# Norms on GpSimd, key blocks in four column tiles, loads by use and chunks of five in a fused attention and Mish kernel

## The chip, the cores and the metric

The kernel runs on 1 core of one Trainium2 chip. The metric is the device time in microseconds of one execution; the time before is the median of three runs, 1579.51 us (1578.79 to 1581.96). The engines are called PE (TensorE), DVE (VectorE), ACT (ScalarE), POOL (GpSimd) and SP (SyncE, which here issues the DMAs). PEld is PE's loading of weights.

## The reference

Everything is FP32. S = 2048 rows of D = 512, 32 query heads of 16 that share one key and one value head, and a hidden layer of F = 1792.

```python
xn = layernorm(x)                                   # no gain, no bias
q  = (xn @ wq) as 32 heads of 16;  k = xn @ wk;  v = xn @ wv
p  = softmax(q @ k.T / 4)                           # over all 2048 keys
s  = concat_heads(p @ v) @ wo
h  = xn @ w1 + b1
g  = silu((h * tanh(softplus(h))) @ w2)             # Mish between two products
out = x + s * g
```

## The kernel before

**Precision.** Most operands are kept as a high and a low FP32R part (`hi_pool` or an ACT copy makes the high part, `sub` the low one), and a product of two such operands is three PE products (`TERMS`). The key and value projection is done in plain FP32 with `wkf`, a weight tile in which the key's 16 columns are repeated six times, columns 48 to 63 are zero, and the value's 16 stand last; the trace shows each FP32 product as two records.

**Work units.** Rows are handled in four chunks of 512 (c = 0 to 3), and heads in sets of four. `NU = 32` pairs of chunk and head set, each with 16 key tiles, make `NS = 512` steps s. In a step, `e_one` makes four score products (`e`) that ACT turns into exponentials (`pt`), `m_one` makes some four products (`m`) whose maxima DVE takes for a later set (`mb`), and `pv` adds the `pt` of two steps before to the output, as four column tiles of 32.

**Groups.** Between these, PE works through *groups* of products that share one PSUM bank (`xps`): a query block (12 products, `q_group`), a block of the first factor (12, `m1_group`), a third of a second-factor product (15, 15 and 12, `m2_groups`), an output block (12, `wo_groups`). `queue` holds them in order, `qqueue` the query groups with the steps from which they may begin; `begin` takes the first that is ready, and goes past a waiting output group to the next first-factor group. `waves` puts one chunk of a group into two steps: the upper halves of its products (64 rows of the contraction) in one, the lower halves in the other, each beside `e` and `m` products that use the other half of PE's rows. `chunk_size` cuts a group into equal chunks of at most `XMAX = 8`, so 12 are 6 + 6 and 15 are 8 + 7; either way a group takes four steps. `m_sides` decides how many `m` stand on which side. After the maxima are all taken, 20 steps (`LEAD`) before the end, the last steps run in pairs with two groups at a time.

**Weights.** `items` has a list for each tag: `wq` (query), `ws` (first factor), `wb` and `wx` (second factor and output). `load` issues the next load of a tag when its place in the ring is free and one of two raw buffers is; `pump` calls it for every tag in the order of the dictionary (wq, ws, wb, wx), and the lead-in's planner does the same. `split` makes the two parts: in the lead-in with an ACT copy and a subtraction on POOL, later both on POOL. Split weights are kept in DRAM and come back ready in later chunks.

**The lead-in.** Before step 0 a planner writes the order of all engines by hand: tasks with an engine, a duration, what they depend on and a priority; at each turn the task that can start first is issued (`best`). `norm_a`, `norm_b` and `norm_c` turn a chunk's sums into `rstd` and `nbias` (DVE, ACT, DVE); DVE gathers the sums of chunks 0 to 2 (`stats`), ACT those of chunk 3 (`stats_a`). `x_scale` applies them, `x_transpose` turns the tiles on PE, `x_copy` brings them to `xf`. Then `k_proj` makes key block c with four accumulating products; `k_high` (ACT) and `k_low` (DVE) write the keys `ks`, `v_copy`, `v_transpose` and `v_out` the values. `m` products of a key block can begin when its `k_low` is done (`kready`); the order over query set and key block is in `MSEQ`. Where PE would wait more than 0.35 us, it does three products of a group ("X"; one group more may begin per 13 us after 18 us) or a warm-up product that nobody reads (`keep_warm`). The lead-in ends when 40 `m` products on each half are out and the row maxima of the first set have been moved (`c_rows`).

Of the kernel before, what the change touches and what calls it, by code (L numbers as in the profile page):

```python
# [14 lines left out]
F32 = mybir.dt.float32  # L15
# [65 lines left out]
class Item:  # L81
    def __init__(self, tag, key, src):
        self.tag, self.key, self.src = tag, key, src
        self.raw = self.tile = None
        self.step = None
        self.users = 0


class Group:
    def __init__(self, mms, post, items=(), after=(), pre=None, start=None, wo=None, alloc=None):  # L90
        self.mms, self.post, self.items, self.after, self.pre = mms, post, items, after, pre
        self.start, self.wo, self.alloc = start, wo, alloc
        self.done = None
        self.m1 = None
        self.dve = False
        self.per = None
        for i in items:
            i.users += 1
# [26 lines left out]
def block_kernel(ctx: ExitStack, tc: tile.TileContext, x, wq, wk, wv, wo, w1, b1, w2, out):  # L125
# [127 lines left out]
    def norm_a(z):  # L253
        if z.start >= A_LO:
            dve.tensor_scalar(ve[:, z], mvs[:, z, 1], 1.0 / D, EPS, op0=ALU.mult, op1=ALU.add)
        else:
            dve.tensor_scalar(ve[:, z], mvs[:, z, 1], EPS, None, op0=ALU.add)
# [5 lines left out]
    def norm_c(z):  # L263
        r, h = rstd[:, z], hv[:, z]
        stt(h, ve[:, z], -0.5, r, ALU.mult, ALU.mult)
        mul(dve, h, h, r)
        stt(r, h, 1.5, r, ALU.add, ALU.mult)
        if z.start >= A_LO:
            mul(dve, nbias[:, z], nbias[:, z], r)
        else:  # L270
            stt(nbias[:, z], mvs[:, z, 0], -1.0, r, ALU.mult, ALU.mult)
# [39 lines left out]

    kp_of = {}
    vp_of = {}

    def k_proj(c, dts):
# [15 lines left out]
    def v_copy(c):  # L331
        vt_of[c] = sb.tile([P, C], F32, tag=f"y{(2, 3, 1, 2)[c]}", name=f"vt{c}", bufs=1)[0:32]
        act.activation(vt_of[c], kp_of[c][96:128], AF.Copy)
# [9 lines left out]
    load_x(0)  # L343
    wkv = sb.tile([P, C], F32, tag="qf", name="wkv", bufs=1)
    wkv = wkv[:, 0:2 * NDT * DH].rearrange("p (a t n) -> p a t n", a=2, t=NDT)
    sp.dma_start(wkv[:, 0], wk.rearrange("(t p) n -> p t n", p=P))
    sp.dma_start(wkv[:, 1], wv.rearrange("(t p) n -> p t n", p=P))
    for j in range(8):
        if j != 3:
            pool.tensor_copy(wkf[:, :, DH * j:DH * (j + 1)], wkv[:, j // 7])  # L350

    timed = {}
# [103 lines left out]
    def load(tag):  # L456
# [14 lines left out]
        elif n - k < NRAW[tag] and raws[-RAWS] is not None and raws[-RAWS] <= step[0]:  # L471
# [8 lines left out]
            todo[tag][1] += 1  # L480

    def pump():
        for tag in items:
            while arrived(tag):
                split(tag)
            load(tag)

# [8 lines left out]
    def prepare():  # L496
        for n in range(min(2 if step[0] < NS - LEAD else 8, len(queue))):
            if queue[n].pre and queue[n].pre():
                queue[n].pre = None

    def begin():
        prepare()
# [10 lines left out]
        if g.start:  # L513
            g.start()
        if g.alloc:
            ps = g.alloc()
        else:
            ps = ps_x.tile([P, 512], F32, tag="x", name="xps")
# [114 lines left out]

    def chunk_size(n):
        return -(-n // -(-n // XMAX)) if n else 0

    def waves(h, em, new):
# [4 lines left out]
        if not cur["chunk"] and (not new or cur["g"] is None and not begin()):  # L642
            mms = []
        else:
            g = cur["g"]
            mms = cur["chunk"] or g.mms[cur["n"]:cur["n"] + chunk_size(len(g.mms) - cur["n"])]
        second = bool(cur["chunk"])
# [6 lines left out]
        xs = deque(mms)  # L654
        swap = k % 2 and not second
        relay = None
# [346 lines left out]
    for c in range(NC):  # L1003
        for k in range(3):
# [13 lines left out]
            queue.extend(g2)  # L1018
    queue.extend(wo_groups(NC - 1))

    pt_of = {}
# [50 lines left out]
    def m_sides(h, k, second):  # L1072

        tot = 4 + (0 if k % 2 == 0 else -1 if second else 1)
        tot = min(tot, 64 * NU - sum(m_next))
# [5 lines left out]
        if k == 6 and abs(off) > 1:  # L1081
            n -= 1 if off > 0 else -1
        n = max(min(n, hi), lo)
        return n, tot - n
# [217 lines left out]
    for c0, c1 in ((0, 1), (1, 2), (2, 3), (3, 4)):  # L1302
        z = slice(4 * c0, 4 * c1)
        na = task("DVE", 0.2, lambda z=z: norm_a(z), st[z], prio=c0 and 1)
        nb = task("ACT", 0.45, lambda z=z: norm_b(z), [na])
        nrm = task("DVE", 0.8, lambda z=z: norm_c(z), [nb], prio=2 * c0 and 1)
        for c in range(c0, c1):
# [39 lines left out]
            kus = 0.9  # L1347
            k0 = kp = task("PE", kus, lambda c=c: k_proj(c, (0,)), xs)
            for dt in range(1, 4):
                kp = task("PE", kus, lambda c=c, dt=dt: k_proj(c, (dt,)), [kp], lat=0.0)  # L1350
            kv_done = kp
# [37 lines left out]
    while True:  # L1389
# [24 lines left out]
        when(s)  # L1414
        for tag in items:
            load(tag)
# [31 lines left out]
        elif k == "J":  # L1448
# [5 lines left out]
            else:  # L1454
                gap[0] = 0
                if not plan["POOL"]:
                    act_jobs(1)
# [29 lines left out]
    for s in range(NS + 2000):  # L1487
        inm = s < NS - LEAD
        if inm or cur["chunk"]:
# [4 lines left out]
            def em(k, second):  # L1494
# [3 lines left out]
                r = [[], []]  # L1498
                for op in EM if k % 2 == 0 or second else EM[::-1]:
                    if op == "M" and y:  # L1500
# [67 lines left out]
```

## Time and profile before

| | before |
|---|---|
| median of 3 runs | 1579.51 us |
| the profiled execution's own time | 1578.89 us |
| its span | 1577.1 us |
| granted PE clock | 1.000 |
| PE, DVE, ACT, POOL busy | 99%, 85%, 83%, 40% of the span |
| the first set of `pv` products | at 87.01 us |

A busy row of the profile gives, for a group of instructions, the line, the engine, the operation, what is written from what, and the count; then the busy time in us and the mean duration in ns. A row of the timeline gives the start and the time that it spans in us, then the same; what ended the engine's idle time before it stands in square brackets. A stretch gives its length and then the busy time of each engine with its number of instructions.

### The profile page before, as it was taken

What the parts mean: (1) busy time and instruction counts of PE and PEld (TensorE: products, weight loads), DVE (VectorE), ACT (ScalarE), POOL (GpSimd) and SP (SyncE); (2) the same over time, 40 slices, a digit from 0 to 9 for tenths busy, and PEclk for the clock granted to TensorE, in tenths of its full rate; (3) what the DMA queues carried; (4) which work ended last, traced back from release to release, by engine and by line L of the source; (5) the groups of instructions that cost most, each with busy time, mean ns of one, the idle gap of its engine ahead of it and who ended that gap; (6) DMA issues with size and microseconds to landing.
All of it is one profiled execution on the core that took longest, in us unless ns stands there. A gap on an engine that the chain in (4) does not pass through costs nothing.

```text
span 1577.1 us, 31648 instructions
## 1 busy us (share of the span) xinstructions
PE 1565.6 (99%) x11717; PEld 842.5 (53%) x11717; DVE 1343.6 (85%) x2339; ACT 1306.6 (83%) x2515; POOL 627.5 (40%) x641
## 2 busy tenths in 40 slices
PE   9999999999999999999999999999999999999998
PEld 5455555555555555555555555555555555555554
DVE  8998888889989888888998988888889998888832
ACT  7588788798998778878989887887898878789886
POOL 3476266275474105503515320471251515126412
PEclk9999999999999999999999999999999999999999
DMA  6333231142321314122032232221332213032020
GB/s 195 94 118 112 65 99 44 55 125 85 121 93 48 102 33 149 45 69 81 26 99 66 60 97 68 84 60 26 116 98 85 74 40 110 19 111 58 15 81 28
DMA packets 74666, 124.31 MB, mean 79 GB/s; under 512 B 21520, under 2 KB 35344, under 8 KB 74512
## 3 DMA queue, kind: packets, MB, share of 16 engines
q1 hardware_dynamic: 74512, 122.29, 25.1%
q8 instruction: 93, 1.52, 0.4%
q14 instruction: 61, 0.50, 0.1%
HBM read 74.78 MB, written 26.21 MB: 64 GB/s over the span
## 4 chain that ended last, share of the span: by engine, by line
PE 96%; DVE 3%; ACT 1%; DMA 0%; issue 0%; SPq 0%; ACTq 0%; DVEq 0%
PE xps L118 44%; PE pv L1126 32%; PE e L1039 9%; PE m L1060 8%; DVE mb L1064 2%; PE kp L319 1%; PE xps L114 0%; PE late L118 0%; ACT pt L1041 0%; PE xp L287 0%; PE late L1039 0%; DMA xin<-in_dram 0%; PE wop L118 0%; PE late L114 0%; PE wop L114 0%
## 5 line engine op out<-in xcount | busy, mean ns | idle before, releaser
L1064 DVE TENSOR_REDUCE mb<-m 128x1 f32<-128x512 f32 x2048 | 1274.2, 683 | 172.2 <-PE m L1060 148.8
L1041 ACT ACTIVATE pt<-e 128x512 f32<-128x512 f32 x2018 | 1061.7, 602 | 221.1 <-PE e L1039 213.3
L1060 PE MATMUL m<-ks,qt 48*128 48x512 f32 (+1 forms) x2048 | 830.3, 420 | 1.3 <-DVE mb L1064 0.4
L1039 PE MATMUL e<-qt,ks 64*128 64x512 f32 x2018 | 740.4, 401 | 0.5 <-ACT pt L1041 0.3
L1126 PE MATMUL pv<-pt,vaug 128*32 128x512 f32 x4096 | 543.0, 604 | 0.0
L1060 PEld LDWEIGHTS m<-ks,qt 48*128 48x128 f32 (+1 forms) x2048 | 372.4, 185 | 59.5 <-DVE mb L1064 21.5
L1039 PEld LDWEIGHTS e<-qt,ks 64*128 64x128 f32 x2018 | 373.1, 186 | 17.1 <-ACT pt L1041 5.7
L118 PE MATMUL xps<-wbs,act 64*128 64x512 f32 x1248 | 338.1, 407 | 0.2
L118 PEld LDWEIGHTS xps<-wbs,act 64*128 64x128 f32 x1248 | 217.5, 185 | 173.9 <-ACT pt L1041 101.6
L118 PE MATMUL xps<-xt,ws 64*128 64x512 f32 x1104 | 306.1, 410 | 0.3 <-DVE y L851 0.2
L118 PEld LDWEIGHTS xps<-xt,ws 64*128 64x128 f32 x1104 | 190.2, 185 | 182.7 <-ACT pt L1041 116.5
L172 POOL TENSOR_SCALAR t<-t 128x512 f32<-128x512 f32 x56 | 34.5, 616 | 400.3 <-ACT t L784 400.1
L1126 PEld LDWEIGHTS pv<-pt,vaug 128*32 128x32 f32 x4096 | 81.8, 108 | 137.9 <-issue 129.6
L162 POOL TENSOR_TENSOR hb<-hb,t 128x512 f32<-128x512 f32 x56 | 72.2, 1289 | 69.2 <-ACT t L797 54.2
L118 PE MATMUL xps<-xt,wq 64*128 64x512 f32 x336 | 93.1, 410 | 0.0
L118 PEld LDWEIGHTS xps<-xt,wq 64*128 64x128 f32 x336 | 57.9, 185 | 55.4 <-ACT pt L1041 35.2
L118 PE MATMUL xps<-wbs,ot_all 64*128 64x512 f32 x288 | 79.5, 408 | 0.0
L118 PEld LDWEIGHTS xps<-wbs,ot_all 64*128 64x128 f32 x288 | 49.5, 184 | 46.7 <-ACT pt L1041 29.3
L162 POOL TENSOR_TENSOR hb<-hb,u 128x512 f32<-128x512 f32 x56 | 72.4, 1292 | 4.4
L162 POOL TENSOR_TENSOR u<-u,t 128x512 f32<-128x512 f32 x56 | 71.9, 1284 | 4.7
L162 POOL TENSOR_TENSOR act<-hb,act 128x512 fp32r<-128x512 f32 x55 | 70.9, 1290 | 4.6
L157 POOL TENSOR_SCALAR qh<-qf 128x512 fp32r<-128x512 f32 x15 | 9.3, 622 | 104.8 <-ACT qf L716 69.4
(146 smaller groups left out, 959.4 us busy)
## 6 DMA issues: line engine op xcount, KB each, us to landing
wbs<-w SPq DMA_DIRECT2D x36, 512.0 KB
ws<-w SPq DMA_DIRECT2D x35, 512.0 KB
qt<-qh SPq DMA_DIRECT2D x256, 32.0 KB
wq<-wq SPq DMA_DIRECT2D x14, 512.0 KB
w<-wbs SPq DMA_DIRECT2D x14, 512.0 KB
wbs<-wo SPq DMA_DIRECT2D x12, 512.0 KB
rawws<-in_dram SPq DMA_DIRECT2D x21, 256.0 KB
rawwb<-in_dram SPq DMA_DIRECT2D x20, 256.0 KB
```

The source lines that it names most:

```text
L118: i = self.pe.matmul(ps, self.lhs()[o], self.rhs()[o], start=(self.k == 0 and self.halves == 0), stop=(self.k == self.tot - 1 and self.hal ...
L157: pool.tensor_scalar(o, i, 1.0, 0.0, op0=ALU.mult, op1=ALU.add)
L162: eng.tensor_tensor(out=o, in0=a, in1=b, op=op)
L172: pool.tensor_scalar(o, o, lim, 0.0, op0=ALU.min, op1=ALU.max)
L319: pe.matmul(kp_of[c], wkf[:, dt], xf_of[c][dt // 2][:, dt % 2], start=(dt == 0), stop=(dt == 3))
L1039: pe.matmul(e, ks[o:o + 64, P * k:P * (k + 1)], q[o:o + 64, p], start=True, stop=True)
L1041: r = act.activation(pt, e, AF.Exp, scale=0.25)
L1060: pe.matmul(m, q[o, p, P * t:P * (t + 1)], ks[o, C * kb:C * (kb + 1)], start=True, stop=True)
L1064: r = dve.reduce_max(out=mb_of[v][:, kb, z:z + 1], in_=m, axis=AX.X)
L1126: pe.matmul(o[32 * j:32 * j + 32], vaug[:, k], pt, start=(k == 0), stop=(k == 15))
```

## The change

It has four parts.

1. **Norms.** For chunks 2 and 3 `norm_a` and `norm_c` are issued on POOL, as products of two tensors and scalar operations, and the planner has them as POOL tasks. Where the planner held timed work and jobs back while POOL had any task, it now does so while one is due.
2. **Key blocks 1 to 3.** `k_part` makes, for each half of 256 columns, four products at once, one for each quarter of the contraction, each into 32 rows of one bank (the last 32 columns of `wkf`: 16 of the key, 16 of the value). `k_stage` copies the bank to SBUF on ACT, and `k_sum` adds the four quarters and repeats the key with one product by a matrix of identity blocks, `ksum`. POOL makes this matrix from the identity with a memset and 28 small copies. Block 0 stays as it is.
3. **Loads by use.** Each item gets the number of the first group in the queue that uses it (`use`; query items 8n − 7), and `load` is called for the tags in the order of their next item's number.
4. **Fives.** When a group of 15 begins while the groups before the first output group of chunk 0 leave more than one step to spare (`spare_steps`), it is cut into three chunks of five. `m_sides` and the order in a step treat five as an even number: four `m`, two on each side.

```diff
+        self.use = 0
+        self.most = XMAX
     def norm_a(z):
-        if z.start >= A_LO:
+        if z.start >= 8:
+            charge(0.25)
+            pool.tensor_scalar(ve[:, z], mvs[:, z, 1], 1.0 / D if z.start >= A_LO else 1.0, EPS, op0=ALU.mult, op1=ALU.add)
+        elif z.start >= A_LO:
...
     def norm_c(z):
-        r, h = rstd[:, z], hv[:, z]
+        r, h, b = rstd[:, z], hv[:, z], nbias[:, z]
+        if z.start >= 8:
+            charge(1.1)
+            pool.tensor_tensor(out=h, in0=ve[:, z], in1=r, op=ALU.mult)
+            pool.tensor_tensor(out=h, in0=h, in1=r, op=ALU.mult)
+            pool.tensor_scalar(h, h, -0.5, 1.5, op0=ALU.mult, op1=ALU.add)
+            pool.tensor_tensor(out=r, in0=h, in1=r, op=ALU.mult)
+            if z.start < A_LO:
+                pool.tensor_scalar(b, mvs[:, z, 0], -1.0, 0.0, op0=ALU.mult, op1=ALU.add)
+            pool.tensor_tensor(out=b, in0=b, in1=r, op=ALU.mult)
+            return
...
+    def k_part(c):
+        kq = ps_v.tile([P, C], F32, tag="v", name=f"kq{c}")
+        for h in range(2):
+            z = slice(C // 2 * h, C // 2 * (h + 1))
+            for dt in range(NDT):
+                pe.matmul(kq[32 * dt:32 * dt + 32, z], wkf[:, dt, P - 32:P], xf_of[c][dt // 2][:, dt % 2, z], start=True, stop=True)
+        kq_of[c] = kq
+
+    def k_stage(c):
+        vt_of[c] = sb.tile([P, C], F32, tag=f"y{(2, 3, 1, 2)[c]}", name=f"vt{c}", bufs=1)
+        act.activation(vt_of[c], kq_of[c], AF.Copy)
+
+    def k_sum(c):
+        kp_of[c] = ps_v.tile([P, C], F32, tag="v", name=f"kp{c}")
+        pe.matmul(kp_of[c], ksum, vt_of[c], start=True, stop=True)
...
+    ksum = wkv[:, P:2 * P]
...
+    pool.memset(ksum, 0.0)
+    for dt in range(NDT):
+        for j in range(8):
+            if j != 3:
+                pool.tensor_copy(ksum[32 * dt:32 * dt + 32, DH * j:DH * (j + 1)], ident[32 * dt:32 * dt + 32, 32 * dt + DH * (j // 7):32 * dt + DH * (j // 7 + 1)])
...
+    def by_use():
+        return sorted(items, key=lambda g: items[g][todo[g][1]].use if todo[g][1] < len(items[g]) else 10 ** 6)
+
     def pump():
         for tag in items:
             while arrived(tag):
                 split(tag)
+        for tag in by_use():
             load(tag)
...
+    def spare_steps():
+
+        n = next((n for n, g in enumerate(queue) if g.wo is not None), None)
+        if n is None or queue[n].wo:
+            return 0
+        due = 16 * 8 * (queue[n].wo + 1) + 9
+        return due - step[0] - 13 - 4 * (1 + n + sum(32 * (16 - k) - LEAD - 20 < due for k in range(1, len(qqueue) + 1)))
...
+        if len(g.mms) == 15 and spare_steps() > 1:
+            g.most = 5
...
-    def chunk_size(n):
-        return -(-n // -(-n // XMAX)) if n else 0
+    def chunk_size(n, most):
+        return -(-n // -(-n // most)) if n else 0
...
-        swap = k % 2 and not second
+        swap = k % 2 and k > 5 and not second
...
+    for n, g in enumerate(queue):
+        for i in g.items:
+            i.use = i.use or n
+    for n, i in enumerate(items["wq"]):
+        i.use = 8 * n - 7
...
-        tot = 4 + (0 if k % 2 == 0 else -1 if second else 1)
+        tot = 4 + (0 if k % 2 == 0 or k == 5 else -1 if second else 1)
...
+        if k == 5:
+            n = 2
...
+    def pool_due():
+        return any(all(d.end is not None for d in k.deps) for k in plan["POOL"])
...
-        if k <= step[0] and busy[0] + E0 < t + 0.5 and not plan["POOL"]:
+        if k <= step[0] and busy[0] + E0 < t + 0.5 and not pool_due():
...
-        na = task("DVE", 0.2, lambda z=z: norm_a(z), st[z], prio=c0 and 1)
+        na = task("POOL" if c0 >= 2 else "DVE", 0.3, lambda z=z: norm_a(z), st[z], prio=c0 and 1)
         nb = task("ACT", 0.45, lambda z=z: norm_b(z), [na])
-        nrm = task("DVE", 0.8, lambda z=z: norm_c(z), [nb], prio=2 * c0 and 1)
+        nrm = task("POOL" if c0 >= 2 else "DVE", 1.6 if c0 >= 2 else 0.8, lambda z=z: norm_c(z), [nb], prio=2 * c0 and 1)
...
+                kq = task("PE", 1.0, lambda c=c: k_part(c), xs)
+                kg = task("ACT", 0.6, lambda c=c: k_stage(c), [kq])
+                bank("v", 1, kq, [kg])
+                k0 = kp = task("PE", 1.0, lambda c=c: k_sum(c), [kg])
```

More of the change, by code (lines that the diff above doesn't have):

```diff
@@ L312, in block_kernel @@
     kp_of = {}
+    kq_of = {}
     vp_of = {}
+    def k_part(c):
[11 more added lines that the diff above has]
+        pe.matmul(kp_of[c], ksum, vt_of[c], start=True, stop=True)
     def k_proj(c, dts):
@@ L331, in v_copy @@
     def v_copy(c):
-        vt_of[c] = sb.tile([P, C], F32, tag=f"y{(2, 3, 1, 2)[c]}", name=f"vt{c}", bufs=1)[0:32]
+        if c == 0:
+            vt_of[c] = sb.tile([P, C], F32, tag=f"y{(2, 3, 1, 2)[c]}", name=f"vt{c}", bufs=1)
+        vt_of[c] = vt_of[c][0:32]
         act.activation(vt_of[c], kp_of[c][96:128], AF.Copy)
@@ L645, in waves @@
             g = cur["g"]
-            mms = cur["chunk"] or g.mms[cur["n"]:cur["n"] + chunk_size(len(g.mms) - cur["n"])]
+            mms = cur["chunk"] or g.mms[cur["n"]:cur["n"] + chunk_size(len(g.mms) - cur["n"], g.most)]
         second = bool(cur["chunk"])
@@ L1346, in block_kernel @@
                 xs += [qp]
[L1347 to L1350, printed above, removed]
+            if c == 0:
+                k0 = kp = task("PE", 0.9, lambda c=c: k_proj(c, (0,)), xs)
+                for dt in range(1, 4):
+                    kp = task("PE", 0.9, lambda c=c, dt=dt: k_proj(c, (dt,)), [kp], lat=0.0)
+            else:
+                kq = task("PE", 1.0, lambda c=c: k_part(c), xs)
+                kg = task("ACT", 0.6, lambda c=c: k_stage(c), [kq])
+                bank("v", 1, kq, [kg])
+                k0 = kp = task("PE", 1.0, lambda c=c: k_sum(c), [kg])
             kv_done = kp
@@ L1414, in block_kernel @@
         when(s)
-        for tag in items:
+        for tag in by_use():
             load(tag)
@@ L1455, in block_kernel @@
                 gap[0] = 0
-                if not plan["POOL"]:
+                if not pool_due():
                     act_jobs(1)
@@ L1498, in em @@
                 r = [[], []]
-                for op in EM if k % 2 == 0 or second else EM[::-1]:
+                for op in EM if k % 2 == 0 or k == 5 or second else EM[::-1]:
                     if op == "M" and y:
```

## The prediction

> **What bounds the kernel now.** I read the page first, then the timeline of the first 160 us, then the stretches between the moments at which the key blocks become usable. The page:
>
> ```profile
> span 1577.1 us, 31648 instructions
> PE 1565.6 (99%) x11717; PEld 842.5 (53%) x11717; DVE 1343.6 (85%) x2339; ACT 1306.6 (83%) x2515; POOL 627.5 (40%) x641
> PE 96%; DVE 3%; ACT 1%; DMA 0%; issue 0%; SPq 0%; ACTq 0%; DVEq 0%
> ```
>
> PE carries 96% of the chain that ended last. DVE's 3% is some 47 us, to be sought where PE waits for DVE: in the lead-in, the only stage in which the norms and the key blocks lie. Its stretches, cut where a key block became usable (columns: us, PE, PEld, DVE, ACT and POOL busy, granted clock, DMA):
>
> ```profile
> 24.80:37.60 12.80, 12.76 (x49) 6.28 (x49) 12.05 (x22) 11.36 (x28) 4.55 (x5) 1.00 0.45 144
> 37.60:50.60 13.00, 12.99 (x49) 6.28 (x48) 12.51 (x26) 9.76 (x25) 6.24 (x6) 1.00 0.44 142
> 50.60:62.70 12.10, 11.66 (x49) 5.79 (x48) 11.73 (x20) 6.31 (x14) 3.08 (x3) 1.00 0.42 131
> 62.70:73.10 10.40, 9.69 (x40) 5.00 (x40) 9.84 (x18) 3.22 (x6) 6.17 (x7) 1.00 0.11 26
> 73.10:78.90 5.80, 5.46 (x24) 2.98 (x24) 5.70 (x13) 2.29 (x4) 5.54 (x6) 1.00 0.17 49
> sum 54.10, PE 52.56 PEld 26.33 DVE 51.82 ACT 32.95 POOL 25.57; mean PE 10.51 PEld 5.27 DVE 10.36 ACT 6.59 POOL 5.11
> ```
>
> DVE works 51.82 of these 54.10 us, so two engines are full at once. DVE reduces the score maxima, 80 of them before the regular steps may begin, and PE makes the key blocks that release them. The end of the lead-in in the timeline:
>
> ```profile
> 54.66 1.12 PE L319 MATMUL kp<-xf,wkf 128*128 128x512 f32 x2
> ...
> 59.11 1.13 PE L319 MATMUL kp<-xf,wkf 128*128 128x512 f32 x2
> 60.28 0.69 ACT L324 ACTIVATE ks<-kp,kone 112x512 fp32r<-112x512 f32 x1 [5.03 <-PE kp L319]
> 60.70 1.29 DVE L1064 TENSOR_REDUCE mb<-m 128x1 f32<-128x512 f32 x2 [0.19 <-PE m L1060]
> 61.90 0.74 DVE L237 SCALAR_TENSOR_TENSOR ks<-ks,ksgn,kp 112x512 fp32r<-112x512 f32 x1
> 63.23 0.69 DVE L1064 TENSOR_REDUCE mb<-m 128x1 f32<-128x512 f32 x1 [0.59 <-PE m L1060]
> 66.96 6.06 DVE L1064 TENSOR_REDUCE mb<-m 128x1 f32<-128x512 f32 x10
> 73.05 0.27 DVE L1093 TENSOR_REDUCE mp<-mb 128x16 f32<-128x64 f32 x1
> ```
>
> Key block 3 takes 5.6 us from its first product to the ACT copy. At 61.9 DVE has nothing left but that block's low part; it then waits for the first maxima product, and from 63.23 reduces without a gap, 0.61 us each, until the row maxima at 73.05. Whatever brings block 3 forward brings the start of the steps forward, so far as DVE has finished its earlier reductions.
>
> **The three key blocks.** Each block now costs PE four full FP32 products (two records each). The price without interleaved work is in block 0's rows, that of four column tiles in the steady loop's, and that of the whole in the group:
>
> ```profile
> 17.02 3.59 PE L319 MATMUL kp<-xf,wkf 128*128 128x512 f32 x8
> 87.01 1.06 PE L1126 MATMUL pv<-pt,vaug 128*32 128x512 f32 x8
> L319 PE MATMUL kp<-xf,wkf 128*128 128x512 f32 x24 | 13.4, 640 | 0.0
> 59.11 0.30 PEld L319 LDWEIGHTS kp<-xf,wkf 128*128 128x128 f32 x2 [0.24 <-issue]
> ```
>
> A full product is 3.59/4 = 0.90 us; four column tiles of 512 columns are 1.06. Eight tiles of 256 columns stream the same columns, so 1.06 too; with no overlap among tiles they would be 3.59. The new chain is 1.06, the ACT copy (0.69, as the copy above), the summing product 0.90, and an issue gap of 0.24 before each PE part: 3.1 instead of 5.6, so 2.5 us less to each block. The summing product waits for the copy; maxima products can stand between them, as they stand between the four products now. PE gives up 13.4 − 3 × (1.06 + 0.90 + 0.48) = 6.1 us. ACT gets 3 × 0.69 = 2.1 us; what hides that is its slack, 1.4 us in the first stretch, 3.2 and 5.8 in the next two. In the first it is short: there the copy delays block 2's scaling, but DVE has maxima of block 1 left to reduce.
>
> **The norms.** Chunks 2 and 3 now cost DVE these places:
>
> ```profile
> 28.11 1.29 POOL L162 TENSOR_TENSOR wq<-rawwq,wq 128x512 fp32r<-128x512 f32 x1 [4.23 <-ACT wq L421]
> 28.40 1.01 DVE L237 SCALAR_TENSOR_TENSOR hv<-ve,rstd 128x4 f32<-128x4 f32 x1
> 29.92 0.68 DVE L1064 TENSOR_REDUCE mb<-m 128x1 f32<-128x512 f32 x1
> 45.28 0.19 DVE L255 TENSOR_SCALAR ve<-mvs 128x4 f32<-128x4 f32 x1
> 46.77 0.15 DVE L237 SCALAR_TENSOR_TENSOR hv<-ve,rstd 128x4 f32<-128x4 f32 x1
> 47.43 0.68 DVE L1064 TENSOR_REDUCE mb<-m 128x1 f32<-128x512 f32 x1
> ```
>
> The same operation took 1.01 us beside a POOL product and 0.15 without one. Leaving DVE saves 1.52 (28.40 to 29.92) + 0.19 + 0.66 (46.77 to 47.43) = 2.4 us. POOL gets seven or eight tiny operations per chunk; the nearest rows are the weight copies and the variance beside them:
>
> ```profile
> 7.12 1.31 POOL L350 COPY wkf<-wkv 128x64 f32<-128x64 f32 x7 [1.35 <-DMA wkv<-in_dram]
> 7.63 0.17 DVE L257 TENSOR_SCALAR ve<-mvs 128x4 f32<-128x4 f32 x1
> ```
>
> 0.19 each: seven operations for chunk 2 and six for chunk 3 make 1.3 and 1.1 us, 0.2 to 0.4 more on the chain than five of DVE's 0.17 to 0.19. [...] The sum doesn't hang on it: chunk 3's maxima are wanted only after DVE has worked off block 2's. On POOL, which works in order, weight splits stand behind the norm while it waits for ACT's squares; they feed groups, not the key blocks.
>
> The 28 copies that build the summing matrix add 28 × 0.19 = 5.3 us on POOL, from 8.4 to 14, where it is idle until its next work:
>
> ```profile
> 19.02 1.27 POOL L162 TENSOR_TENSOR ws<-rawws,ws 128x512 fp32r<-128x512 f32 x1 [10.59 <-ACT rstd L260]
> ```
>
> DVE's chunk 0 norm lies beside them; the 0.17 at 7.63 shows no loss beside such copies, and the bound is one copy ahead of each of five operations, 0.95 us. I take 0.2.
>
> **Sum of the lead-in.** Ceiling: all DVE idle time (54.10 − 51.82 = 2.3) and the norms (2.4), 4.7 us. Block 3's own chain gives 2.5, and DVE is then ready for it: its 61.99 becomes 59.6 by the norms alone. DVE's remaining gaps beside the fewer PE parts should close in part. I take 3.0, less 0.2 for the copies: **2.8 us** (0 to 4.7).
>
> **Groups.** PE's freed 6.1 us, less some 2.8 for the shorter lead-in, go into waiting groups:
>
> ```profile
> L114 PE MATMUL xps<-xt,ws 128*128 128x512 f32 x15 | 4.8, 430 | 0.0
> L114 PE MATMUL xps<-xt,early 128*128 128x512 f32 x15 | 4.6, 425 | 0.6 <-ACT hb L776 0.3 <-ACT qf L716 0.3
> L114 PE MATMUL xps<-xt,wq 128*128 128x512 f32 x12 | 3.9, 430 | 0.3 <-ACT hb L776 0.3
> ```
>
> That is 42 products at (4.8 + 4.6 + 3.9)/42 = 0.32 us; 3.3 us is ten more. With the 3 already begun one group more is finished: five and a bit beside the first, where four and a quarter are now. The begin rule (one per 13 us after 18) allows it. That is four steps ahead in the loop. Two stretches of the loop, cut at the starts of pv sets, and the first of the two steps that hold no group's product between their pv sets:
>
> ```profile
> 124.07:148.42 24.35, 24.33 (x191) 13.19 (x189) 20.21 (x34) 20.99 (x42) 17.45 (x18) 1.00 0.50 164
> 148.42:159.86 11.44, 11.44 (x91) 6.03 (x89) 9.42 (x17) 8.79 (x19) 1.52 (x2) 1.00 0.11 31
> 472.54:475.25 2.71, 2.57 (x18) 1.06 (x16) 2.37 (x5) 2.71 (x7) 0.44 (x1) 1.00 0.67 201
> ```
>
> The first is two groups of 15, eight steps of 3.04; the second one of 12, four of 2.86. The spare-step rule, worked out for the present kernel at its first group of 15 (step 16, 23 groups and 4 query groups before the first output group), gives 124 − 16 − 4 × 27 = 0: no group would be split. One group ahead gives 4, and two are split. The same work is now 24.35 + 11.44 = 35.8 us, and becomes twelve steps with five. None is in the trace; a five has 5 + 2 products against 4 + 2, as many in its longer half as a six, so 2.86, between the bare step's 2.71 and the 3.04 above. 12 × 2.86 = 34.3: **1.5 us** saved (3.3 saved at 2.71, 0.7 lost at 3.04; nothing if no group is ahead).
>
> **Loads by use** add no instruction; on SP's queue they put the second factor's weights ahead of first-factor weights needed later. Two bare steps leave little to win, about a us; a late load would cost one bare step, 2.7. I take 0.
>
> Sum: 2.8 + 1.5 = 4.3 us off the profiled execution's own 1578.89, so 1574.6. That run stands 0.6 below the median of its three, and against the median of 1579.5 it is **1575.2**.
>
> **The rivals.**
> 1. *No group ahead.* X work only fits where PE waits more than 0.35 us; if DVE's closer pace or a pending evacuation leaves no such holes, no group is split: 2.8 alone, 1576.7. The warm-up products in the present lead-in speak against it; the 2.8 us that the lead-in loses, in its emptiest part, for it. 0.16.
> 2. *ACT takes it back.* ACT is busy 11.36 of 12.80 in the first stretch, and the squares of chunk 3 yield to everything. The copies push them back by 2.1 us, and block 3 comes 0.4 earlier: about 1579. Against: ACT idles 5.8 us in the third stretch. 0.11.
> 3. *Slower: POOL's queue.* POOL works in order, and a group's first four products are one piece of 3.9 us:
>
> ```profile
> 67.44 0.61 POOL L172 TENSOR_SCALAR t<-t 128x512 f32<-128x512 f32 x1 [3.99 <-ACT t L784]
> 68.13 0.62 POOL L787 TENSOR_SCALAR u<-t 128x512 f32<-128x512 f32 x1
> 68.84 1.29 POOL L162 TENSOR_TENSOR u<-u,t 128x512 f32<-128x512 f32 x1
> 70.20 1.28 POOL L162 TENSOR_TENSOR hb<-hb,u 128x512 f32<-128x512 f32 x1
> ```
>
> If both halves of chunk 3's norm stand behind such a piece, block 3 comes 7.8 − 2.5 = 5.3 us later, no group is ahead, and the time is 1584.8. It decides from 2.8 us of delay, where it eats the lead-in's gain. For it: POOL works 6.24 of 13 us in the second stretch. Against: the planner sees POOL as an engine, and holds timed work back while a norm is due. 0.12. I leave 0.03 for slower by something unnamed, such as late loads.
>
> **How the numbers follow.** Forecast 0.58, rivals 0.16, 0.11 and 0.12, 0.03 left. About 0.2%, 3.2 us, is what a measurement of this kernel can tell from no change. The forecast passes it in 19 of 20 cases, rival 1 in half: faster 0.55 + 0.08 = 0.63; same 0.03 + 0.08 + 0.11 = 0.22; slower 0.15. The forecast's terms at their good ends (4.7 and 3.3) give 1571.5, with a load's wait won 1571.0; rivals 1 and 2 end near 1579, with a bare step lost 1580.0. That leaves out rival 3 and the unnamed.
>
> **What would show it.** The row maxima near 70 us and the first e product near 76; DVE's busy share up to there at 97% or more without norms of chunks 2 and 3; kp's three blocks in some 2 us of PE each; 12 to 15 more products at L114's line before the steps; six to nine steps with five. Wrong: block 3's low part later than 60.5, more bare steps, a step with five over 3 us, or chunk 3's norm ending past 50.

## The result, and the profile after

| | before | after | forecast |
|---|---|---|---|
| median of 16 runs each | 1578.99 us | 1576.52 us | 1575.2 (1571.0 to 1580.0) |
| ratio to before, 95% interval | | 0.9984 (0.9977 to 0.9991) | |
| the profiled execution's own time, its span | 1578.89, 1577.1 us | 1576.55, 1574.4 us | 1574.6 |
| first maxima reduction on DVE | 24.80 us | 25.26 us | |
| row maxima | 73.05 us | 72.31 us | near 70 |
| first `e` product | 78.95 us | 78.16 us | near 76 |
| first set of `pv` products | 87.01 us | 86.26 us | |
| the twelve steps that end at 148.42 (before), 146.28 (after) | 35.8 us | 34.4 us | 34.3 |

The change took 2.5 us off, 0.16%: clear of no change by its interval, but less than the 0.2% (3.2 us) that the prediction took as the least that can be told from none. Of this, 0.75 us came at the first `pv` set, where 2.8 were forecast, 1.4 in the steps with five (1.5 forecast), and some 0.4 in small pieces along the loop. In some executions of these kernels the granted clock falls to 0.50, in the profiles below for some 3.4 us or for 6.8; where a profile caught this, the text or the clock in its stretches says so.

The page of the changed kernel, with the same three rows:

```profile
span 1574.4 us, 31742 instructions
PE 1562.6 (99%) x11738; PEld 842.0 (53%) x11738; DVE 1341.1 (85%) x2329; ACT 1307.8 (83%) x2518; POOL 633.7 (40%) x683
PE 95%; DVE 4%; ACT 1%; DMA 0%; issue 0%; SPq 0%; ACTq 0%; DVEq 0%
```

DVE's share of the chain that ended last rose from 3% to 4%. Within its first 90 us DVE's reductions of the maxima have 45.0% where they had 26.1%, and PE's key products 8.5% where they had 17.7%: the lead-in was bound by PE and DVE in turn, and is now bound more by DVE. Its stretches, from the first reduction to the first `e` product (columns as in the prediction):

```profile
25.26:36.37 11.11, 11.11 (x63) 6.14 (x63) 10.60 (x18) 10.70 (x26) 2.44 (x7) 1.00 0.49 156
36.37:47.50 11.13, 10.65 (x56) 5.39 (x55) 9.30 (x17) 8.46 (x21) 5.44 (x6) 1.00 0.47 151
47.50:61.16 13.66, 13.46 (x72) 7.92 (x70) 13.52 (x25) 10.84 (x24) 11.76 (x17) 1.00 0.29 95
61.16:72.31 11.15, 10.26 (x44) 5.31 (x42) 10.52 (x19) 3.10 (x6) 5.97 (x6) 1.00 0.27 74
72.31:78.16 5.85, 5.50 (x24) 3.10 (x24) 5.75 (x13) 2.21 (x4) 5.55 (x6) 1.00 0.02 5
sum 52.90, PE 50.98 PEld 27.86 DVE 49.68 ACT 35.31 POOL 31.15; mean PE 10.20 PEld 5.57 DVE 9.94 ACT 7.06 POOL 6.23
```

DVE works 49.68 of 52.90 us. Its idle time is 3.2 us; it was 2.3. Most of it lies in the second stretch, 1.8 of 11.13. The timeline of DVE there, and of the end of the lead-in:

```profile
41.33 1.29 DVE L1123 TENSOR_REDUCE mb<-m 128x1 f32<-128x512 f32 x2 [1.24 <-PE m L1119]
43.21 1.29 DVE L1123 TENSOR_REDUCE mb<-m 128x1 f32<-128x512 f32 x2 [0.59 <-PE m L1119]
44.41 0.74 DVE L239 SCALAR_TENSOR_TENSOR ks<-ks,ksgn,kp 112x512 fp32r<-112x512 f32 x1
...
47.66 13.58 DVE L1123 TENSOR_REDUCE mb<-m 128x1 f32<-128x512 f32 x22
61.16 0.74 DVE L239 SCALAR_TENSOR_TENSOR ks<-ks,ksgn,kp 112x512 fp32r<-112x512 f32 x1
62.48 2.48 DVE L1123 TENSOR_REDUCE mb<-m 128x1 f32<-128x512 f32 x4 [0.59 <-PE m L1119]
72.31 0.27 DVE L1154 TENSOR_REDUCE mp<-mb 128x16 f32<-128x64 f32 x1
```

Block 2's low part comes at 44.41, 5.4 us earlier than before (49.82). Block 3's, at 61.16, comes only 0.7 earlier; ahead of it DVE reduces 22 times without a gap. What PE did before the hole at 41.33:

```profile
38.04 0.67 PE L1119 MATMUL m<-ks,qt 64*128 64x512 f32 x2
38.82 1.05 PE L1434 MATMUL warm<-qt 128*128 128x512 f32 x2
39.80 1.07 PE L336 MATMUL kq<-xf,wkf 128*32 128x256 f32 x16
40.80 0.49 PE L1119 MATMUL m<-ks,qt 64*128 64x512 f32 x2
41.61 1.13 PE L345 MATMUL kp<-vt,wkv 128*128 128x512 f32 x2 [0.32 <-ACT vt L341]
```

Between two pairs of `m` products, 2.8 us apart, stand two warm-up products and the key products. And ACT at the same time, then POOL at chunk 3's norm:

```profile
40.96 0.60 ACT L341 ACTIVATE vt<-kq 128x512 f32<-128x512 f32 x1 [2.07 <-PE kq L336]
41.46 0.71 ACT L248 ACTIVATE junk<-xin,nbias 128x512 f32<-128x512 f32 x1
...
45.66 0.72 ACT L248 ACTIVATE junk<-xin,nbias 128x512 f32<-128x512 f32 x1
```

```profile
47.08 1.28 POOL L164 TENSOR_TENSOR early<-rawws,early 128x512 fp32r<-128x512 f32 x1 [4.08 <-ACT early L461]
48.45 0.19 POOL L258 TENSOR_SCALAR ve<-mvs 128x4 f32<-128x4 f32 x1
49.26 0.20 POOL L272 TENSOR_TENSOR hv<-ve,rstd 128x4 f32<-128x4 f32 x1 [0.62 <-ACT rstd L266]
...
50.38 0.20 POOL L278 TENSOR_TENSOR nbias<-nbias,rstd 128x4 f32<-128x4 f32 x1
```

ACT, whose queue is written in a fixed order, waits 2.07 us for block 2's key products with chunk 3's squares behind that copy; the squares end at 46.5 us (43.6 before). Then the norm stands behind a weight subtraction on POOL, and ends at 50.6 (47.5 before).

### The profile page after: what moved, and what is told of

It reads as the page before. It is cut to its first block, busy times and chain, and to the rows that moved or that the text cites. A ratio compares the mean times of both kernels' runs of the same rounds, so it can differ in the third digit from the quotient of the medians.

```text
span 1574.4 us, 31742 instructions
## 1 busy us (share of the span) xinstructions
PE 1562.6 (99%) x11738; PEld 842.0 (53%) x11738; DVE 1341.1 (85%) x2329; ACT 1307.8 (83%) x2518; POOL 633.7 (40%) x683
## 4 chain that ended last, share of the span: by engine, by line
PE 95%; DVE 4%; ACT 1%; DMA 0%; issue 0%; SPq 0%; ACTq 0%; DVEq 0%
PE xps L120 44%; PE pv L1187 32%; PE e L1098 9%; PE m L1119 7%; DVE mb L1123 3%; PE late L120 1%; PE xps L116 0%; ACT pt L1100 0%; DMA xin<-in_dram 0%; PE late L1098 0%; PE kp L351 0%; PE wop L120 0%; PE xp L302 0%; PE late L116 0%; PE wop L116 0%
## 5 line engine op out<-in xcount | busy, mean ns | idle before, releaser
L174 POOL TENSOR_SCALAR t<-t 128x512 f32<-128x512 f32 x56 | 34.4, 615 | 395.1 <-ACT t L838 394.9
```

The lines of the kernel that those rows point to most:

```text
L174: pool.tensor_scalar(o, o, lim, 0.0, op0=ALU.min, op1=ALU.max)
```

## The experiments

Two theories were open. **A:** the lead-in's gain was lost where chunk 3's norm came 3 us later, and with it block 3. **B:** DVE's reductions and its holes set the lead-in, whenever block 3 comes. The measure is DVE's way from its first reduction to the row maxima, 48.25 us before and 47.05 after, since the first reduction itself shifts between executions with the landing of the input tiles. In each diff the changed kernel is the old side.

**No fives.**

```diff
-        if len(g.mms) == 15 and spare_steps() > 1:
+        if False:
```

> The changed kernel, but groups of fifteen are always two steps of eight and seven. Theory (the lead-in gave 0.75 us, the fives 1.4): the lead-in is as in the changed kernel, the first sets of pv products stand at 86.3 us; between the steps at 111.9 and 146.3 us the twelve steps of 2.86 us become eight of seven and eight products at 3.04, and four steps without products appear later at 2.7 us each or more: 8 x 3.04 + 4 x 2.71 = 35.2 against 34.4, so 0.8 us slower, and up to 2.7 us slower at the 3.18 us that the later bare step took: 1577.3 to 1579.2, about 1578.0. Rival (the fives are worth nothing, all of the gain is the lead-in's): 1576.5 within 0.3.

1580.26 us, ratio to before 1.0011 (1.0002 to 1.0019): slower than the kernel before, and 3.7 us above the changed one. The lead-in is the same (first `pv` set 86.43). The four spare steps became four more bare ones (six where the changed kernel has two), but they cost more than expected. Two of them with what follows, in stretches of that kernel:

```profile
229.45:232.16 2.71, 2.57 (x19) 1.05 (x17) 2.38 (x5) 2.71 (x7) 2.55 (x3) 1.00 0.23 50
232.16:235.70 3.54, 3.54 (x27) 2.01 (x25) 2.73 (x6) 3.17 (x7) 2.01 (x3) 1.00 0.23 53
315.54:318.70 3.16, 2.79 (x19) 1.19 (x18) 2.80 (x5) 2.49 (x6) 2.83 (x4) 1.00 0.23 93
318.70:327.72 9.02, 9.02 (x67) 4.70 (x67) 7.20 (x13) 7.97 (x17) 5.24 (x6) 1.00 0.28 80
```

The first bare step takes 2.71 us, and the step of eight behind it 3.54 where others take 3.07. The second takes 3.16, and the three steps of six behind it 9.02 where three others take 8.55. Each of these two bare steps thus has a wake of about 0.5 us, which both ranges expected for this run missed. It isn't a rule: in the run that follows, the step behind ten bare ones in a row takes 3.06 us, no longer than others of eight. What makes the wake stays open. In this kernel a group finished ahead is worth less than nothing unless its steps are spread.

**Loads in the old order.**

```diff
     def by_use():
-        return sorted(items, key=lambda g: ...)
+        return list(items)
```

> The changed kernel, but the weight loads are issued in the fixed order of the four lists as before, not by their use. Theory (the order of loads is worth nothing, the two steps without products stand at the same places in both traces): first sets, fives and bare steps as in the changed kernel, 1576.5 within 0.4. Rival (loads by use feed the group that the lead-in finishes more, or keep bare steps away): one to four bare steps more, at about 3 us each and 0.7 for the three steps behind each, 1577.5 to 1580.

1585.92 us, ratio 1.0043 (1.0029 to 1.0057): some 9 us worse than the changed kernel. The theory, and the 0 in the prediction, fell. The loads of the second factor on SP's queue, in this kernel and then in the changed one (first and last start at the end of each row's times):

```profile
L516 SPq DMA_DIRECT2D rawwb<-in_dram x4: 430/431/608, 108.2 to 136.6; - x4
```

```profile
L516 SPq DMA_DIRECT2D rawwb<-in_dram x4: 340/361/384, 64.1 to 85.3; - x4
```

One group ahead, the group of 15 is due at 111.7 us. In the old order its weights are issued from 108 us on, behind first-factor weights, so ten bare steps stand from 111.69 to 138.73, eight more come later, and no step has five. What was not done there has to be done at the end; from the last `pv` set to the end, this kernel and then the changed one:

```profile
1556.90:1584.60 27.70, 19.08 (x94) 12.77 (x92) 9.21 (x16) 10.23 (x20) 8.20 (x8) 0.93 0.10 39
```

```profile
1558.25:1574.40 16.15, 10.94 (x58) 6.16 (x57) 7.28 (x14) 4.56 (x10) 2.53 (x2) 0.99 0.17 65
```

**Norms back on DVE.**

```diff
-        na = task("POOL" if c0 >= 2 else "DVE", ...
+        na = task("DVE", ...           # norm_c and the bodies likewise
```

> The changed kernel, but the norms of chunks 2 and 3 are on VectorE as before; key blocks, loads and fives stay. Theory (DVE is the bound of the lead-in, and of the 2.4 us that the norms freed on it 1.2 were lost again to a hole at 40 to 44 us): the 2.4 us come back, chunk 3's norm no longer waits for POOL and ends about 1.5 us earlier, and the first set of pv products goes back from 86.3 to about 87.0 us; the key blocks alone are worth nothing. Time 1577.0 to 1577.5. Rival (POOL's queue holds block 3, and block 3 holds the end): the first set comes 0.5 to 1.5 us earlier than in the changed kernel, 1575.0 to 1576.0.

1577.54 us, 0.9995 (0.9987 to 1.0004). The way is 49.77 us, 2.7 more than the changed kernel's and 1.5 more than before the change; the first `pv` set stands at 89.08. Seven more group products are done before the first `pv` set (84 against 77, the first query group left out), so 18 steps have five and win part of it back. DVE's norm of chunk 3 in the timeline, two of POOL's operations beside it, and the sum row of the stretches of its way:

```profile
51.17 0.80 DVE L239 SCALAR_TENSOR_TENSOR hv<-ve,rstd 128x4 f32<-128x4 f32 x1
52.01 0.54 DVE L164 TENSOR_TENSOR hv<-hv,rstd 128x4 f32<-128x4 f32 x1
52.58 0.16 DVE L239 SCALAR_TENSOR_TENSOR rstd<-hv,rstd 128x4 f32<-128x4 f32 x1
52.78 0.46 DVE L164 TENSOR_TENSOR nbias<-nbias,rstd 128x4 f32<-128x4 f32 x1
```

```profile
50.67 1.28 POOL L164 TENSOR_TENSOR act<-hb,act 128x512 fp32r<-128x512 f32 x1
52.61 0.62 POOL L841 TENSOR_SCALAR u<-t 128x512 f32<-128x512 f32 x1
```

```profile
sum 49.77, PE 47.81 PEld 25.94 DVE 47.05 ACT 34.41 POOL 27.61; mean PE 11.95 PEld 6.49 DVE 11.76 ACT 8.60 POOL 6.90
```

Of the tiny operations the long ones end when POOL's do, the first at 51.97 (POOL's at 51.95), the last at 53.24 (53.23), and take 0.46 to 0.80 us, where the one at 52.58 takes 0.16. Why they end together these rows don't show. The 3.1 us that DVE works more (47.05 against 43.94 in the changed kernel, whose sum row follows with the next run) are more than the whole difference in the way. Block 3's high part, too, comes 2.8 us later after the first reduction (37.6 against 34.8), so this run doesn't part A from B. The key blocks without the norms don't shorten the lead-in. The theory's 87.0 was too mild, its direction right.

**Four-product key blocks.**

```diff
-            if c == 0:                 # k_proj, else k_part, k_stage, k_sum
+            if True:
```

> The changed kernel, but all four key blocks by four full products each as before (28 copies for the sum's matrix stay); norms on POOL, loads and fives stay. PE has 6.8 us more to do in the lead-in, ACT three copies of 0.7 us less. Theory (DVE is the bound; norms on POOL give most of the 0.75 us): the first set of pv products at 86.3 to 86.8 us, but one group less is finished in the lead-in, so there is nothing for the fives to spread: they do not appear, or bare steps take their place, 1577.5 to 1578.5. Rival (the key blocks' chain is what gave the 0.75 us): the first set at 87.0 us or later, 1578.2 to 1579.2.

1577.32 us, 0.9995 (0.9986 to 1.0003). The way is 47.09, as in the changed kernel, so with the norms on POOL the lead-in has all of its gain without the new key blocks. On A and B it says nothing: chunk 3's norm ends at 46.6 us, four earlier than in the changed kernel, but the longer key chain takes that back, and block 3's high part is done 35.0 us after the first reduction (34.8 in the changed kernel). The missing group (66 products against 77, counted as above) takes all fives away; the bare steps are the two of before. The key blocks' part of the gain is the group, and with it the fives. The sum rows of the way, of before, of the changed kernel and of this one:

```profile
sum 48.25, PE 47.05 PEld 23.35 DVE 46.08 ACT 30.60 POOL 19.97; mean PE 11.76 PEld 5.84 DVE 11.52 ACT 7.65 POOL 4.99
```

```profile
sum 47.05, PE 45.48 PEld 24.76 DVE 43.94 ACT 33.10 POOL 25.60; mean PE 11.37 PEld 6.19 DVE 10.98 ACT 8.27 POOL 6.40
```

```profile
sum 47.09, PE 46.17 PEld 22.80 DVE 44.33 ACT 29.18 POOL 20.88; mean PE 11.54 PEld 5.70 DVE 11.08 ACT 7.30 POOL 5.22
```

**Chunk 3's sums sooner.** (The planner's unit of rank is 0.4 us, so the edit is smaller than its text says.)

```diff
-    sums = [task("ACT", 0.8, ..., prio=2.8) ...   # means and squares likewise
+    sums = [task("ACT", 0.8, ..., prio=2.2) ...
```

> The changed kernel, but ScalarE's sums and squares of chunk 3 get a rank of 2.2 us in place of 2.8 behind the other work, so that they come before some of its copies. In the changed kernel its squares ended at 46.5 us (43.6 before the change), and the norm of chunk 3 then stood behind a weight subtraction of 1.3 us on POOL and ended at 50.6 (47.5 before). Theory (block 3 came only 0.7 us earlier because its norm came 3 us later, and VectorE's hole at 40 to 44 us stands in the same stretch): the norm ends at 47 to 49 us, block 3's low part at 58.5 to 60.5 rather than 61.2, the first set of pv products at 85.0 to 85.8, time 1575.2 to 1576.0. Rival (VectorE's reductions, which run without a gap from 47.7 to 61.2 us, bound it): the low part moves, the first set does not by more than 0.2, time 1576.5 within 0.3.

1576.53 us, 0.9992 (0.9984 to 1.0001): the rival's time, but neither range's picture. Chunk 3's norm ended at 47.3, but block 3's low part came at 63.0 and the way took 49.74. The profile shows a fall of the clock in it:

```profile
39.00:46.00 7.00, 6.67 (x28) 2.81 (x21) 5.33 (x9) 5.38 (x13) 5.27 (x7) 1.00 0.36 91
46.00:52.80 6.80, 6.74 (x17) 3.27 (x17) 4.19 (x9) 2.57 (x4) 4.09 (x8) 0.50 0.15 41
```

From 46.0 to 52.8 us the granted clock is 0.50. From 39.6 to 46 us seven of PE's products are warm-up products, and two pairs of `m` products waited 0.9 us behind them. That the clock is what lengthened the way is likely, since the same ranks with the clock at 1.00 gave 46.76 (the third run of the next group, whose fillers also have another bank). The other ten executions took 1575.6 to 1582.5 us, so the fall is probably in some of them only.

**No filler products; fillers in the groups' bank; both with the sums.** A warm-up product takes one of the three banks of the `m` products. Its rows in the changed kernel:

```profile
L1434 PE MATMUL warm<-qt x8: 387/446/502, 35.8 to 61.0; 128*128 128x512 f32 x8
its engine sat idle before it (us, times) until:
  DVE mb L1123: 1.0, 3
```

```diff
                 else:
-                    keep_warm()
-                    T["PE"] = s + 0.25
+                    T["PE"] = s + 0.1            # no filler products
```

```diff
-                    keep_warm()
+                    pe.matmul(ps_x.tile([P, C], F32, tag="x", name="warm"), ...
```

> The changed kernel, but where TensorE has nothing to do in the lead-in no filler (warm-up) product is issued: the two at 38.8 us and the one at 49.0 go; those ahead of two fixed places stay. In the changed kernel the fillers waited 1.0 us for VectorE, because they take one of the three PSUM banks of the row-maximum products, and what stood behind them on TensorE (block 2's key products, the next pair for VectorE) waited too. Measure: VectorE's way from its first reduction (25.26 us) to the row maxima (72.31), 47.05 us in the changed kernel, 48.25 before. Theory (the hole of 2.2 us in VectorE at 40 to 44 us comes of these fillers): the way becomes 46.0 to 46.6 us, the time 1575.5 to 1576.1. Rival 1 (the hole comes of the key products and their sum waiting for ScalarE): 47.0 within 0.2, 1576.5. Rival 2 (without fillers the granted clock falls to 0.50 for some 6.7 us, as it did in the run with chunk 3's sums sooner from 46.0 to 52.7 us): 48.5 to 50 us, 1577.5 or more.

> The changed kernel, but the filler products of the lead-in write to the weight groups' PSUM bank in place of a row-maximum bank, so that they don't wait for VectorE. Theory (the bank is what made them wait): VectorE's way from first reduction to row maxima 46.0 to 46.6 us in place of 47.05, granted clock 1.00 throughout, time 1575.5 to 1576.1. Rival (the group bank is no freer, the fillers wait for ScalarE's copy of it, or the hole has another cause): 46.9 to 47.3 us, 1576.3 to 1576.8.

> The changed kernel with both edits: ScalarE's sums and squares of chunk 3 ranked at 2.2 us as in the run with chunk 3's sums sooner, and the filler products in the weight groups' bank. In that run chunk 3's norm ended at 47.3 us in place of 50.6, but fillers waited for VectorE and products behind them for the fillers (3.2 us), and the granted clock fell to 0.50 from 46.0 to 52.7 us; VectorE's way from first reduction to row maxima was 49.74 us. Theory (these two ate the gain of the earlier norm): with the fillers out of the way the clock stays at 1.00 and the way is 45.0 to 46.3 us, the time 1574.3 to 1576.0, with the fives as they come. [...] Rival 2 (VectorE's reductions bound it as in the changed kernel): 46.8 to 47.2 us.

Without fillers the way was 46.30 us, as the theory of its text had it. But the edit also took those between 9 and 21 us, which that text overlooks; the profile has the clock at 0.50 around 17 us and the first reduction at 27.17. Time 1577.07, 0.9982 (0.9973 to 0.9991), no better than the changed kernel. With the fillers in the groups' bank, of which there is only one, each early filler waited for the one before, so that the first five took 2.70 us where they took 1.59, and together they held the first groups back; at 51.6 us PE waited another 0.91 us for ACT's copy of that bank. First reduction 27.10, way 47.5, 1578.73 us, 0.9998 (0.9989 to 1.0007). With both edits the first reduction stood at 26.68, and the time was 1580.40 us, 1.0006 (0.9997 to 1.0014), spread from 1577.59 to 1584.60. But its profile, of an execution of 1577.88 us and with the clock at 1.00, parts A from B. Block 3's high part in the ACT timeline:

```profile
59.23 0.69 ACT L356 ACTIVATE ks<-kp,kone 112x512 fp32r<-112x512 f32 x1 [1.22 <-PE kp L345]
```

It is done 33.2 us after the first reduction, 1.55 earlier than in the changed kernel (by the clock of the span at the same time, 59.92 against 60.05; it is DVE that began later). The low part still stands behind reductions until 62.22, 2.3 us later, and the way is 46.76, only 0.3 shorter. So an earlier block 3 wins little; B holds. All thirteen profiles say the same: block 3's low part begins 0.65 to 2.3 us after its high part is done, right behind a reduction, and the row maxima follow 11.14 to 11.30 us after it. In none did DVE wait for block 3's high part. What the fillers cost, these three don't show cleanly; the next does.

**No late fillers; key times mended; the changed kernel again.**

```diff
                 else:
-                    keep_warm()
+                    if s < 30.0:
+                        keep_warm()
```

```diff
-                kq = task("PE", 1.0, ...          # in addition to the edit above
+                kq = task("PE", 0.8, ...
-                k0 = kp = task("PE", 1.0, ...
+                k0 = kp = task("PE", 0.6, ...
```

> The changed kernel without the three filler products behind 30 us (at 38.8, 39.4 and 49.0); those at 8 to 21 us stay. The run without any filler had VectorE's hole at 42 us at 0.48 in place of 1.24 us and its way from first reduction to row maxima at 46.30 in place of 47.05 us, but had lost the early fillers too, and its granted clock was 0.50 at 16 to 18 us, its first reduction 1.9 us late. Theory (the late fillers wait for a row-maximum bank and hold back the next products for VectorE): the way is 46.1 to 46.5 us, the clock 1.00 throughout, the first reduction at 24.6 to 25.5, the time 0.6 to 0.9 below the changed kernel's in the same comparison, about 1575.8 against a before of 1579.0. Rival (the late fillers are needed for the clock): 0.50 in some stretch behind 40 us, the way 48 or more, time 1577 or more.

> As the run without late fillers, and the times that the planner gives to the column-tiled key products and to their sum are 0.8 and 0.6 us in place of 1.0 and 1.0, so that it places the high and low parts of the key blocks, and what comes behind them, sooner in each engine's order (in the changed kernel block 3's products began at 56.4 us and its high part was done at 60.05, while its low part stood behind reductions until 61.16). Theory (VectorE's reductions and its holes set the way, the key blocks are not late): the way from first reduction to row maxima changes by less than 0.4 us against the run without late fillers, 46.0 to 46.7. Rival (a block's place in the order is what holds VectorE): 45.0 to 45.9 us, and the time 0.5 to 1.2 below that run's.

> The changed kernel itself, unaltered, so that the two runs beside it have it on the same chip, and for a second look at where its first reduction falls. Theory (the first reduction at 25.26 us, 0.46 later than before, is the landing of the input tiles, not the 28 small copies on POOL): it falls anywhere from 24.4 to 25.5 us with the first variance on VectorE from 7.2 to 8.2, and the distance between the two is 17.2 to 17.3 us as in all runs whose clock stayed at 1.00; its way to the row maxima is 47.0 to 47.1 us; the time about 2.5 below the kernel before. Rival (the copies cost it): the first variance at 8.0 or later again, in each run that has the copies.

On the same chip: the changed kernel 1576.35 us, 0.9982 (0.9972 to 0.9991); without late fillers 1575.64, 0.9976 (0.9967 to 0.9985); with the key times mended too 1575.44, 0.9974 (0.9964 to 0.9984). The last two are faster than the kernel before, and below the changed one in the medians, by 0.7 and 0.9 us; these intervals overlap, but ten of the eleven executions without late fillers and all eight of the last kernel lie below the changed kernel's median. The hole without late fillers, in DVE's timeline, and the sum row of its way:

```profile
40.86 1.29 DVE L1123 TENSOR_REDUCE mb<-m 128x1 f32<-128x512 f32 x2 [0.48 <-PE m L1119]
```

```profile
sum 46.41, PE 44.72 PEld 24.15 DVE 44.05 ACT 32.15 POOL 25.68; mean PE 11.18 PEld 6.04 DVE 11.01 ACT 8.04 POOL 6.42
```

1.24 became 0.48, the way 46.41: DVE works as long as in the changed kernel (44.05) and idles 0.75 less. This profile, against what was expected, has a fall of the clock (0.57 from 64 to 68 us), but there DVE reduces without a gap, and the run with the key times mended, at 1.00 throughout the lead-in, has the same gain. The fillers at 39 to 49 us were thus not needed for the way; whether they make such a fall rarer, one profile of each doesn't show, and the changed kernel with them had one too (below). With the mended key times, which were to bring it sooner, block 3's high part is done 34.7 us after the first reduction, 0.66 later than without them (34.0), and the way is 46.48 all the same: again not block 3. The changed kernel again had a way of 47.07. Its first variance was at 7.94 and its first reduction 17.2 us later; in the runs with the clock at 1.00 up to there and early fillers as before, the first variance lay anywhere from 7.27 to 8.27, all with the 28 copies, and the distance was 17.2 or 17.3. So the 0.46 us at the start are the input's landing, not the copies. This profile of the changed kernel, too, has a fall of the clock:

```profile
76.00:82.00 6.00, 5.22 (x25) 2.63 (x23) 6.00 (x11) 4.39 (x8) 5.75 (x7) 1.00 0.36 101
82.00:86.00 4.00, 3.68 (x22) 2.48 (x18) 3.75 (x7) 3.08 (x7) 3.12 (x4) 0.57 0.16 50
```

If the clock was 1.00 outside the fall and 0.50 in it, 0.57 over 4 us comes to 0.43 × 4 / 0.5 = 3.4 us of it. Its first `pv` set stands at 86.82, 0.56 later than in the other profile of the same kernel, with the row maxima at 72.24 against 72.31.

## Why the prediction was right, and where not

**The total** came within 1.3 us: a gain of 4.3 was forecast and 2.5 measured. Of the two terms one was right and one far too large, and the small pieces of the loop (0.4) weren't in the sum. The range held because it gave the lead-in anything from 0 to 4.7, not because the lead-in was read rightly. Rival 1's 1576.7 comes nearer to the 1576.52 by chance: its mechanism, no group ahead, did not happen.

**The lead-in** (2.8 forecast, 0.75 measured, 1.2 on DVE's way) is the term that was mis-sized. The step that failed is "block 3's own chain gives 2.5, and DVE is then ready for it … DVE's remaining gaps should close in part". The chain did shrink: from its first product at 56.41 to the ACT copy of its high part at 59.36 it took 2.95 us (forecast 3.1). But it began later, because chunk 3's norm ended 3.1 us later. And that was not what decided: with block 3 ready 1.55 us earlier the way shrank by 0.3. The prediction's own rows could have said so: in the kernel before, block 3's high part was done at 60.97 (60.28 and 0.69), and DVE took the low part at 61.90, right behind two reductions. DVE had reductions to do until 61.16 in the changed kernel, not until the 59.6 of the prediction (0.46 of this is the later first reduction), so the lead-in could win only what DVE worked or idled less. DVE's work fell by 2.14 us (46.08 to 43.94; forecast 2.4). Its idle time, from which up to 2.3 were to be won, rose by 0.94 instead. 0.7 of that were the late warm-up products, as the runs without them show: part of PE's freed time went into products that nobody reads and that stood in the queue for a bank. Two of the prediction's own signs of being wrong came true, block 3's low part later than 60.5 and chunk 3's norm past 50, and one sign of being right did not: DVE was busy for 93% of its way to the row maxima (43.94 of 47.05), not 97%.

**The rivals.** What was said of ACT's slack failed: ACT waited 2.07 us in order for the key products with the squares behind it. POOL's queue cost chunk 3's norm some 2 us (squares' end 46.5 to `ve` at 48.45). Rivals 2 and 3 thus both happened, on a smaller scale; together they can have moved the end by little, since block 3 wasn't what DVE waited for.

**The norms' price** held. From `ve` to `nbias` chunk 3's norm took 2.13 us on POOL and ACT (48.45 to 50.58), against 2.23 on DVE and ACT (45.28 to 47.51). POOL's two-input operations took 0.20 us each, DVE's in the kernel before 0.15 to 0.17. **The copies** cost nothing that the runs show; 0.2 was taken.

**The groups** were right in size and mechanism: one group more was finished, two of 15 became twelve steps with five, and these took 34.37 us (forecast 34.3):

```profile
111.91:146.28 34.37, 34.37 (x255) 16.92 (x253) 30.36 (x54) 29.21 (x58) 24.52 (x25) 1.00 0.44 134
```

The count of "six to nine steps with five" in the prediction's last part contradicted its own twelve.

**Loads by use** at 0 fits the two bare steps, which are the same as before, but as a reading it was wrong. They pay for the group that the lead-in finishes early: without them the rest of the change loses 6.5 us to before (1585.92 against 1579.45). Norms, key blocks, loads and fives don't add up; the group ahead costs without the fives and costs more without its loads.

## What to carry to other kernels

When an engine is nearly full, ask what takes off its own work and its own holes; to bring its next input forward by 1.55 us won 0.3 here, and a filler that shared its buffers made new holes (1.24 us on DVE, 0.48 without it). Work finished ahead was worth something here only because what follows was ready (its weights loaded) and spread over the steps, so cost such edits together and undo each one alone to see its share. A step left without work can slow the steps behind it, here by about 0.5 us after two of the bare steps.

## What the runs showed of the hardware that was not expected

In the run with chunk 3's sums sooner PE's granted clock fell to 0.50 while the records had PE busy for 6.67 of the 7.00 us before: seven of the 28 products there were warm-up products, five of them in two rows of single ones that began some 0.55 us apart. What made the clock fall is not shown: in the run with both edits the records have PE busy for 6.75 of the same 7.00 us, and the clock was 1.00 in the 6.80 us behind them. Up to 92 us of the span the falls lasted 6.8 us there and some 3.4 us, worked out as above, in three other profiles (no filler products, no late fillers, the changed kernel again). The changed kernel had one in its second profile (0.57 from 82 to 86 us) and none there in its first (1.00); no run shows why.
